# First key projection by both column halves of four token tiles, and wider spacing of the last attention batches, in a gated two-branch attention kernel

## The chip, the cores and the metric

The kernel runs on one core of a Trainium2 chip. The metric is the device time of one execution, in microseconds (us). Before the change it was 474.53 us, the median of three runs (474.02 to 475.82).

## The reference, cut to what matters

Two attention branches share one input and are mixed by a gate. Branch A is linear attention, branch B a local, dilated one. There are 2048 tokens, width 1024, and 32 heads of 32.

```python
x = A_x                                                # [1, 2048, 1024] bf16
g = sigmoid((x * gate_w).sum(-1, keepdims=True))
# A: q, k, v = split(x @ A_wqkv); phi(t) = where(t > 0, t + 1, exp(t)) + 1e-6
#    kv = phi(k)^T v per head; z = sum of phi(k); o = phi(q) kv / (phi(q) z); a = o @ A_wo
# B: q, k, v = split(x @ B_wqkv); each token attends to 8 earlier ones, 2 apart
#    softmax, times v; b = o @ B_wo
return g * a + (1 - g) * b
```

The change touches the first stage, phi(x @ A's key columns), and the end of branch B's attention, which is done in batches between other matmuls.

## The kernel before: the parts that matter

The keys of A are 2048 x 1024: 16 token tiles of 128 by two column halves of 512, each a sum over 8 steps of 128 (`kt`). That is 256 matmuls of 128 x 512. They need x transposed (`xT`), which DMA transposes bring, and the weights (`WkA[half]`). The loads are written like this:

```python
    WkA = [wpool.tile([P, KT, 512], BF16, name="WkA0", tag="wa")]

    def load_xT(k, t0, t1):
        nc.sync.dma_start_transpose(out=xT[:, 2 * k:2 * k + 2, t0 * P:t1 * P],
                                    in_=rows(x, t0 * P, t1 * P)[:, 2 * k * P:(2 * k + 2) * P])

    for k in range(4):
        (nc.sync if k else nc.scalar).dma_start(
            out=WkA[0][:, 2 * k:2 * k + 2, :],
            in_=A_wqkv[2 * k * P:(2 * k + 2) * P, D:D + 512].rearrange("(kt p) n -> p kt n", p=P))
        for t in (0, 4):
            load_xT(k, t, t + 4)
    for t in range(8, NB):
        nc.sync.dma_start_transpose(out=xT[:, :, t * P:(t + 1) * P], in_=rows(x, t * P, (t + 1) * P))
    WkA += load_w("WkA", A_wqkv, D, "wa", only=(1,))
    # ... the rows of x for the next stage, then more weights
```

The matmuls fill eight accumulation banks, one for each of the first eight token tiles, group `k` of two `kt` steps by group. The other tiles and the second half follow one bank at a time. `phi` empties a bank with one ScalarE exponential and two VectorE instructions.

```python
            warm_up(38)                  # matmuls on a tile of ones, results unused

            first = [bank_k(t) for t in range(8)]
            for k in range(4):
                for t in range(8):
                    for kt in (2 * k, 2 * k + 1):
                        project(first[t], t, kt, 0)
                    if k == 3:
                        phi(work, pk[:, t, 0:512], first[t])
            for half in range(2):
                for t in range(NB):
                    if half == 0 and t < 8:
                        continue
                    pj = bank_k(t)
                    for kt in range(KT):
                        project(pj, t, kt, half)
                    phi(work, pk[:, t, half * 512:(half + 1) * 512], pj)
```

Branch B's attention runs in 40 batches, `scores(g)` and later `pv(g)`, placed between the steps of other matmuls. A step is four 64 x 512 quadrant matmuls. `pv` writes the one `o2` tile, which VectorE has to empty (reciprocals, then multiplications) before the next `pv`.

```python
            for g, (c, m, n) in enumerate(BATCHES):
                p_ = 64 * c + ((43, 55, 75, 86, 97) if c < KT - 1 else (43, 55, 75, 81, 87))[m // 4]
                events.append((p_, lambda g=g: scores(g)))
                events.append((p_ + (14 if c < KT - 1 or m < 8 else 11), lambda g=g: pv(g)))
```

The softmax here doesn't subtract the row's maximum and nothing guards it: scores larger than these inputs give would overflow.

Of the kernel before, what the change touches and what calls it, by code (L numbers as in the profile page):

```python
# [10 lines left out]
BF16 = mybir.dt.bfloat16  # L11
F32 = mybir.dt.float32
# [3 lines left out]
P = 128  # L16
# [23 lines left out]
def kernel(  # L40
# [11 lines left out]
    nc = tc.nc  # L52
    S, D = A_x.shape[1:]
# [5 lines left out]
    def rows(ap, s0, s1):  # L59
        return ap[s0 // 1024, s0 % 1024:(s1 - 1) % 1024 + 1, :]  # L60
# [3 lines left out]
    KT = D // P  # L64
    NB = S // P
# [5 lines left out]
    wpool = ctx.enter_context(tc.tile_pool(name="wpool", bufs=2))  # L71
# [4 lines left out]
    def load_w(name, src, col0, tag, only=(0, 1)):  # L76
        halves = []
        for h in only:
            w = wpool.tile([P, KT, 512], BF16, name=f"{name}{h}", tag=tag)
            c0 = col0 + h * 512  # L80
            nc.sync.dma_start(out=w[:], in_=src[:, c0:c0 + 512].rearrange("(kt p) n -> p kt n", p=P))
            halves.append(w)
        return halves
# [4 lines left out]
    def load_rows(eng, t0, t1):  # L88
        eng.dma_start(out=xrow[:, t0:t1, :], in_=rows(x, t0 * P, t1 * P).rearrange("(t p) d -> p t d", p=P))

    WkA = [wpool.tile([P, KT, 512], BF16, name="WkA0", tag="wa")]

    def load_xT(k, t0, t1):
        nc.sync.dma_start_transpose(out=xT[:, 2 * k:2 * k + 2, t0 * P:t1 * P],  # L94
                                    in_=rows(x, t0 * P, t1 * P)[:, 2 * k * P:(2 * k + 2) * P])

    for k in range(4):
        (nc.sync if k else nc.scalar).dma_start(  # L98
            out=WkA[0][:, 2 * k:2 * k + 2, :],
            in_=A_wqkv[2 * k * P:(2 * k + 2) * P, D:D + 512].rearrange("(kt p) n -> p kt n", p=P))  # L100
        for t in (0, 4):
            load_xT(k, t, t + 4)
    for t in range(8, NB):
        nc.sync.dma_start_transpose(out=xT[:, :, t * P:(t + 1) * P], in_=rows(x, t * P, (t + 1) * P))
    WkA += load_w("WkA", A_wqkv, D, "wa", only=(1,))
    load_rows(nc.sync, 0, 4)
    for t in range(4, NB, 4):
        load_rows(nc.sync, t, t + 4)
# [34 lines left out]
    def phi(work, dst, pj):  # L143
        e = work.tile([P, 512], F32, name="e", tag="e")
        nc.scalar.activation(out=e[:], in_=pj[:], func=ACT.Exp)  # L145
        nc.vector.tensor_scalar(out=e[:], in0=e[:], scalar1=1.0, scalar2=1e-6, op0=ALU.min, op1=ALU.add)  # L146
        nc.vector.scalar_tensor_tensor(out=dst, in0=pj[:], scalar=0.0, in1=e[:], op0=ALU.max, op1=ALU.add)

    with tc.manual_schedule(engines={PE}):

        with ExitStack() as s1:
            ps_1 = s1.enter_context(tc.tile_pool(name="ps_1", bufs=4, space=bass.MemoryType.PSUM))
            junk = s1.enter_context(tc.tile_pool(name="junk", bufs=1))
            work = s1.enter_context(tc.tile_pool(name="work1", bufs=3))

            s1.enter_context(tc.manual_schedule(engines={DVE}))
            pk = big.tile([P, NB, D], BF16, name="pk", tag="pkO")
            def project(pj, t, kt, half):
                nc.tensor.matmul(pj[:], lhsT=xT[:, kt, t * P:(t + 1) * P], rhs=WkA[half][:, kt, :],  # L159
                                 start=(kt == 0), stop=(kt == KT - 1))  # L160

            def warm_up(n):
                warm = ps_1.tile([P, P], F32, name="warm", tag="p1")
                for i in range(n):
                    nc.tensor.matmul(warm[:], lhsT=onesb[:], rhs=onesb[:], start=True, stop=True)


            warm_up(38)

            def bank_k(t):  # L170
                return (ps_1.tile([P, 512], F32, name="pk1_ps", tag="p1") if t & 4 else
                        ps_pj.tile([P, 512], F32, name="pk_ps", tag="pj"))

            first = [bank_k(t) for t in range(8)]
            for k in range(4):
                for t in range(8):
                    for kt in (2 * k, 2 * k + 1):
                        project(first[t], t, kt, 0)
                    if k == 3:
                        phi(work, pk[:, t, 0:512], first[t])  # L180
            for half in range(2):
                for t in range(NB):
                    if half == 0 and t < 8:
                        continue
                    pj = bank_k(t)
                    for kt in range(KT):
                        project(pj, t, kt, half)
                    phi(work, pk[:, t, half * 512:(half + 1) * 512], pj)
# [8 lines left out]
            for t in range(1, NB):  # L197
                side.append(lambda t=t: nc.vector.tensor_tensor(
                    out=zacc[:], in0=zacc[:] if t > 1 else pk[:, 0, :], in1=pk[:, t, :], op=ALU.add))
            side.append(lambda: nc.gpsimd.partition_all_reduce(zrow[:], zacc[:], P, bass_isa.ReduceOp.add))  # L200
            for t in range(NB):
                side.append(lambda t=t: nc.vector.tensor_tensor_reduce(
                    out=gjunk[:], in0=xrow[:, t, :], in1=gw_row[:], scale=1.0, scalar=0.0, op0=ALU.mult,
# [3 lines left out]
            for half in range(2):  # L207
                g_ = junk.tile([P, KT, 512], BF16, name=f"G{half}", tag=f"G{half}")
                G.append(g_)
                for kt in range(KT):  # L210
                    pj = ps_pj.tile([P, 512], F32, name="g_ps", tag="pj")
# [142 lines left out]
        with ExitStack() as s2:  # L354
# [93 lines left out]
            def pv(g):  # L448
                c, m0, n = BATCHES[g]
                pt, base, ns = PT[g % 2], BLOCKS[m0][0], n // 2  # L450
                o2 = ps_o.tile([P, 2, 512], F32, name="o2", tag="o")[:, :, 0:ns * 132] \
                    .rearrange("p a (s i e) -> p a s i e", s=ns, i=4)
                for s_ in range(ns):
                    for i in range(4):
                        for dm in range(2):
                            for par in range(2):
                                m = m0 + 2 * s_ + dm
                                o = BLOCKS[m][0] - base
                                r = slice(64 * par, 64 * par + 64)
                                h = (dm + par) % 2  # L460
                                nc.tensor.matmul(o2[64 * h:64 * h + 64, par, s_, i, :], lhsT=pt[r, i, o:o + 64],  # L461
                                                 rhs=V[r, m, 4 * c + i, :], start=True, stop=True)
                part = m0 >= 8
                if m0 in (0, 8):
                    obs[part] = small.tile([P, 2, 5, P], BF16, name="Ob", tag="Ob")
                Ob = obs[part]
                s0 = m0 // 2 - 4 * part
                rd = small.tile([P, 2, 2, 4, 1], F32, name="rd", tag="rd")
                for a in range(2):
                    nc.vector.reciprocal(out=rd[:, a, 0:ns], in_=o2[:, a, :, :, Dh:Dh + 1])  # L470
                for a in range(2):
                    nc.vector.tensor_tensor(out=Ob[:, a, s0:s0 + ns, :].rearrange("p s (i e) -> p s i e", i=4),
                                            in0=o2[:, a, :, :, 0:Dh],
                                            in1=rd[:, a, 0:ns].broadcast_to([P, ns, 4, Dh]), op=ALU.mult)
                if m0 not in (4, 16):
                    return
                runs = ((0, 1), (1, 4), (2, 3)) if not part else ((8, 1), (9, 4), (10, 4), (17, 1))
                for par in range(2):
                    for m, k in runs:
                        h = (m + par) % 2  # L480
                        q0, w, _ = BLOCKS[m]
                        step = 2 * w if k > 1 else w
                        sl = m // 2 - 4 * part
                        nc.sync.dma_start(
                            out=obd[c][1024 * par + q0:1024 * par + q0 + k * step, :]
                            .rearrange("(s r) d -> r s d", r=step)[0:w],
                            in_=Ob[64 * h:64 * h + w, par, sl:sl + k, :])
                    if part and c == KT - 1:
                        nc.sync.dma_start_transpose(out=OBT[:, c, 1024 * par:1024 * par + 1024],
                                                    in_=obd[c][1024 * par:1024 * par + 1024, :])  # L490
                if part and c < KT - 1:
                    nc.sync.dma_start_transpose(out=OBT[:, c, :], in_=obd[c][0:S, :])

            events = []
            for g, (c, m, n) in enumerate(BATCHES):
                p_ = 64 * c + ((43, 55, 75, 86, 97) if c < KT - 1 else (43, 55, 75, 81, 87))[m // 4]
                events.append((p_, lambda g=g: scores(g)))
                events.append((p_ + (14 if c < KT - 1 or m < 8 else 11), lambda g=g: pv(g)))

            def between(a, b):  # L500
                return [(p_ - a, f) for p_, f in events if a <= p_ < b]
# [12 lines left out]
            for c in range(KT):  # L514
                kts[c] = kpool.tile([P, 2, 1024], BF16, name="kt", tag="kt")
                for hh in range(2):
# [3 lines left out]
                    if 1 <= c <= 2:  # L520
                        t = 2 * (c - 1) + hh
                        nc.sync.dma_start_transpose(out=pqT[0][:, :, t * P:(t + 1) * P],
                                                    in_=pqd[t * P:(t + 1) * P, :])
# [26 lines left out]
        with ExitStack() as s3:  # L550
# [44 lines left out]
            first = [out_part(i, *p_) for i, p_ in enumerate(parts[:7])]  # L595
# [3 lines left out]
            for i, p_ in enumerate(parts):  # L599
# [4 lines left out]
                f = out_part(i, *p_)  # L604
# [33 lines left out]
```

## Time and profile before

| what | value |
|---|---|
| time, median of 3 | 474.53 us |
| the execution that was profiled | 475.77 us, span 474.0 us |
| TensorE busy | 466.4 us of the span |
| first key matmul / next stage starts | 5.80 / 61.90 us |

The profile is of an execution 1.2 us longer than the median.

From the page of the profile of before, the shares of busy time and the chain of work that ended last. TensorE (PE) is nearly always busy, and the rest of the chain is the sync engine's queue (SPq) and a transfer.

```profile
PE 466.4 (98%) x5718; PEld 245.7 (52%) x5750; DVE 277.1 (58%) x601; ACT 168.7 (36%) x271; POOL 25.5 (5%) x88
...
PE 95%; SPq 3%; DMA 1%; issue 1%; ACT 0%
```

From the waits of TensorE in before (engine, line, what it waited for, then us in total, how often, the longest):

```profile
PE pk_ps L159 <- DMA xT<-in_A_x_dram: 0.9, 2, 0.5
PE o L461 <- issue: 0.5, 1, 0.5
```

From the timeline of before, 0 to 14 us (start, duration, engine, line, instruction; in brackets the idle time ahead of it and what ended it). The first two DMA transposes cost the sync engine 1.34 and 1.43 us to issue, and the first key matmul waits 0.45 us for the first of them.

```profile
0.80 2.83 SPq L94 DMA_TRANSPOSE xT<-in_A_x_dram  x2
...
1.12 4.23 PE L165 MATMUL warm<-onesb 128*128 128x128 bf16 x38 [1.12 <-DVE onesb L116]
3.67 0.58 SPq L98 DMA_DIRECT2D WkA<-in_A_wqkv_dram  x1
...
5.80 8.38 PE L159 MATMUL pk_ps<-WkA,xT 128*128 128x512 bf16 x37 [0.45 <-DMA xT<-in_A_x_dram]
```

From the same kernel's timeline of TensorE, 17 to 23 us: the second wait, for token tile 8.

```profile
20.29 2.98 PE L159 MATMUL pk_ps<-WkA,xT 128*128 128x512 bf16 x13 [0.48 <-DMA xT<-in_A_x_dram]
```

From the chain of before, 346 to 361 us (start, duration, what): the end of the attention. 0.54 us pass with no work ("issue": nothing that the profile shows is waited for) ahead of the last value matmuls (`o L461`).

```profile
346.88 0.20 PE s2b L438 x15
...
351.32 0.32 PE o L461 x32
351.64 1.31 PE q_ps L381 x24
352.95 0.54 issue
353.49 0.31 PE o L461 x16
353.80 6.49 PE q_ps L381 x120
360.29 0.32 PE d_ps L579
```

I use two distances below: from the first key matmul to the start of the next stage (`g_ps`), and from this `s2b` at 346.88 to the output stage's first `d_ps` at 360.29, here 13.41 us.

### The profile page before, as it was taken

Reading aid. Unit: us, or ns where it says so; the run is one execution under the profiler, and the core shown is the slowest. Engines: PE = TensorE matmul, PEld = TensorE weight load, DVE = VectorE, ACT = ScalarE, POOL = GpSimd, SP = SyncE. Lnnn points to the kernel's source line nnn. Section 1 sums busy time; section 2 is a strip of 40 time slices with the busy share of each in tenths; the row PEclk is TensorE's granted clock in tenths of the full one; section 3 lists DMA queues with packets and bytes.
Section 4 is the critical chain, followed back from the end, with each engine's and each line's share of the span. In section 5 each row is a group of like instructions: output and inputs, shape, how many; then the busy total and the mean of one; then the engine's idle time right before and its main releaser. Section 6 shows DMA issues by size and latency. Waiting matters only on the chain.

```text
span 474.0 us, 13165 instructions
## 1 busy us (share of the span) xinstructions
PE 466.4 (98%) x5718; PEld 245.7 (52%) x5750; DVE 277.1 (58%) x601; ACT 168.7 (36%) x271; POOL 25.5 (5%) x88
## 2 busy tenths in 40 slices
PE   8999999999999999999999999999999999999997
PEld 5444444445444444445666666666665444444444
DVE  0586689990329999999566676767660049800000
ACT  1343311102433333333555555555551134221121
POOL 2910000500000000001000000000000000000000
PEclk9999999999999999999999999999999999999999
DMA  8999980000644243627326525442563933221111
GB/s 184 189 260 374 347 267 0 0 1 0 215 127 110 93 139 130 154 96 240 112 56 108 104 59 85 99 90 56 92 166 71 198 91 78 68 55 45 34 34 45
DMA packets 98557, 55.41 MB, mean 117 GB/s; under 512 B 69826, under 2 KB 90434, under 8 KB 98498
## 3 DMA queue, kind: packets, MB, share of 16 engines
q1 hardware_dynamic: 93474, 50.10, 41.7%
q10 hardware_dynamic: 5024, 4.46, 2.9%
q8 instruction: 45, 0.74, 0.7%
q14 instruction: 14, 0.11, 0.1%
HBM read 26.10 MB, written 15.86 MB: 89 GB/s over the span
## 4 chain that ended last, share of the span: by engine, by line
PE 95%; SPq 3%; DMA 1%; issue 1%; ACT 0%
PE q_ps L381 26%; PE d_ps L579 12%; PE p_ps L288 12%; PE g_ps L213 12%; PE e_ps L579 11%; PE pk_ps L159 9%; PE p_ps L324 9%; SPq L94 2%; PE o L461 2%; PE s2b L438 2%; DMA xT<-in_A_x_dram 1%; PE kv_ps L233 0%; SPq L98 0%; PE w_ps L276 0%; ACT osb L584 0%
## 5 line engine op out<-in xcount | busy, mean ns | idle before, releaser
L381 PE MATMUL q_ps<-xT,WqB 64*64 64x512 bf16 x1024 | 68.3, 376 | 0.0
L381 PE MATMUL q_ps<-xT,WkB 64*64 64x512 bf16 x1024 | 67.9, 376 | 0.0
L146 DVE TENSOR_SCALAR e<-e 128x512 f32<-128x512 f32 x64 | 27.4, 428 | 64.9 <-ACT e L145 64.9
L288 PE MATMUL p_ps<-WvB,xT 128*128 128x512 bf16 x250 | 57.2, 379 | 0.5 <-issue 0.3
L159 PE MATMUL pk_ps<-WkA,xT 128*128 128x512 bf16 x251 | 55.4, 379 | 1.2 <-DMA xT<-in_A_x_dram 0.9
L213 PE MATMUL g_ps<-pk,xrow 128*128 128x512 bf16 x250 | 54.9, 379 | 0.3
L443 ACT ACTIVATE PT<-s2b 128x928 bf16<-128x928 f32 (+4 forms) x40 | 34.2, 854 | 46.1 <-PE s2b L438 46.1
L445 DVE TENSOR_TENSOR PT<-PT,mask 128x928 bf16<-128x928 bf16 (+4 forms) x40 | 23.6, 590 | 36.9 <-ACT PT L443 36.9
L324 PE MATMUL p_ps<-WqA,xT 128*128 128x512 bf16 x187 | 43.1, 379 | 0.3
L579 PEld LDWEIGHTS <-pqT 128*128 128x128 bf16 x264 | 25.8, 98 | 29.8 <-issue 0.4
L159 PEld LDWEIGHTS <-xT 128*128 128x128 bf16 x256 | 24.8, 98 | 31.5 <-DMA xT<-in_A_x_dram 2.0
L579 PEld LDWEIGHTS <-OBT 128*128 128x128 bf16 x264 | 25.8, 98 | 29.4
L213 PEld LDWEIGHTS <-xrow 128*128 128x128 bf16 x256 | 25.0, 98 | 30.2
L288 PEld LDWEIGHTS <-xT 128*128 128x128 bf16 x256 | 24.6, 98 | 30.0 <-issue 0.9
L381 PEld LDWEIGHTS <-WkB 64*64 64x64 bf16 x1024 | 32.3, 107 | 15.1 <-issue 0.6
L381 PEld LDWEIGHTS <-WqB 64*64 64x64 bf16 x1024 | 31.6, 107 | 15.2 <-issue 0.7
L145 ACT ACTIVATE e<-pk_ps 128x512 f32<-128x512 f32 x32 | 18.9, 597 | 41.6 <-PE pk_ps L159 36.6
L293 ACT CAST tmp<-p_ps 128x512 bf16<-128x512 f32 x32 | 18.8, 590 | 37.5 <-PE p_ps L288 31.2
L579 PE MATMUL d_ps<-WoA,pqT 128*128 128x512 bf16 (+1 forms) x133 | 31.1, 373 | 0.2
L579 PE MATMUL d_ps<-WoB,OBT 128*128 128x512 bf16 (+1 forms) x134 | 31.2, 373 | 0.1
L324 PEld LDWEIGHTS <-xT 128*128 128x128 bf16 x192 | 18.8, 98 | 22.7
L584 ACT ACTIVATE osb<-d_ps,omg 128x512 bf16<-128x512 f32 (+1 forms) x17 | 11.5, 674 | 50.1 <-PE d_ps L579 48.4
(62 smaller groups left out, 512.4 us busy)
## 6 DMA issues: line engine op xcount, KB each, us to landing
vd<-tmp SPq DMA_DIRECT2D x16, 264.0 KB
xrow<-in_A_x_dram SPq DMA_DIRECT2D x4, 1024.0 KB
out_dram<-osb ACTq DMA_DIRECT2D x31, 128.0 KB
pqd<-tmp SPq DMA_DIRECT2D x12, 256.0 KB
WvA<-in_A_wqkv_dram SPq DMA_DIRECT2D x2, 1024.0 KB
WoA<-in_A_wo_dram SPq DMA_DIRECT2D x2, 1024.0 KB
WvB<-in_B_wqkv_dram SPq DMA_DIRECT2D x2, 1024.0 KB
WqA<-in_A_wqkv_dram SPq DMA_DIRECT2D x2, 1024.0 KB
```

The source lines that it names most:

```text
L145: nc.scalar.activation(out=e[:], in_=pj[:], func=ACT.Exp)
L146: nc.vector.tensor_scalar(out=e[:], in0=e[:], scalar1=1.0, scalar2=1e-6, op0=ALU.min, op1=ALU.add)
L159: nc.tensor.matmul(pj[:], lhsT=xT[:, kt, t * P:(t + 1) * P], rhs=WkA[half][:, kt, :], start=(kt == 0), stop=(kt == KT - 1))
L213: nc.tensor.matmul(pj[:], lhsT=xrow[:, t, kt * P:(kt + 1) * P], rhs=pk[:, t, half * 512:(half + 1) * 512], start=(t == 0), stop=(t == NB - 1))
L288: nc.tensor.matmul(st["pj"][:], lhsT=xT[:, kt, t * P:(t + 1) * P], rhs=WvB[half][:, kt, :], start=(kt == 0), stop=(kt == KT - 1))
L293: nc.scalar.copy(out=v[:, half * 16:(half + 1) * 16, 0:Dh], in_=st["pj"][:].rearrange("p (h e) -> p h e", h=16))
L324: nc.tensor.matmul(st["pj"][:], lhsT=xT[:, kt, t * P:(t + 1) * P], rhs=WqA[half][:, kt, :], start=(kt == 0), stop=(kt == KT - 1))
L381: nc.tensor.matmul(banks[o][64 * j:64 * j + 64, :], lhsT=lhsT(r, kt, j), rhs=rhs(r, kt), start=first and kt == 0, stop=kt == KT - 1, skip_ ...
L443: nc.scalar.activation(out=pt[:, :, 0:W_], in_=s2b[:].rearrange("p a b s -> p (a b) s")[:, :, 0:W_], func=ACT.Exp, scale=SCALE)
L445: nc.vector.tensor_tensor(out=pt[:, :, 0:W_], in0=pt[:, :, 0:W_], in1=mask[:, None, base:base + W_].broadcast_to([P, 4, W_]), op=ALU.mult)
L579: nc.tensor.matmul(st["ps"][:, 0:n], lhsT=lhsT, rhs=W[c0 // 512][:, c, c0 % 512:c0 % 512 + n], start=(side == 0 and c == 0), stop=(side == ...
L584: nc.scalar.activation(out=osb[:, 0:n], in_=st["ps"][:, 0:n], func=ACT.Copy, scale=omg[:, tb:tb + 1])
```

## The change

Its intent is to start the first matmul on half as much x, to use each transposed piece for both column halves so that fewer transposes are needed early, and to give VectorE more time between the last batches. Four token tiles by two halves now fill the eight banks. The weights come in eight pieces. Eight steps and nine steps lie between the last batches in place of six and six.

```diff
--- before.py
+++ after.py
@@ -88,21 +88,27 @@
     def load_rows(eng, t0, t1):
         eng.dma_start(out=xrow[:, t0:t1, :], in_=rows(x, t0 * P, t1 * P).rearrange("(t p) d -> p t d", p=P))
 
-    WkA = [wpool.tile([P, KT, 512], BF16, name="WkA0", tag="wa")]
+    WkA = [wpool.tile([P, KT, 512], BF16, name=f"WkA{h}", tag="wa") for h in range(2)]
 
     def load_xT(k, t0, t1):
         nc.sync.dma_start_transpose(out=xT[:, 2 * k:2 * k + 2, t0 * P:t1 * P],
                                     in_=rows(x, t0 * P, t1 * P)[:, 2 * k * P:(2 * k + 2) * P])
 
-    for k in range(4):
-        (nc.sync if k else nc.scalar).dma_start(
-            out=WkA[0][:, 2 * k:2 * k + 2, :],
-            in_=A_wqkv[2 * k * P:(2 * k + 2) * P, D:D + 512].rearrange("(kt p) n -> p kt n", p=P))
-        for t in (0, 4):
-            load_xT(k, t, t + 4)
-    for t in range(8, NB):
+    def load_wk(eng, k, h):
+        eng.dma_start(out=WkA[h][:, 2 * k:2 * k + 2, :],
+                      in_=A_wqkv[2 * k * P:(2 * k + 2) * P, D + 512 * h:D + 512 * h + 512]
+                      .rearrange("(kt p) n -> p kt n", p=P))
+
+    load_wk(nc.scalar, 0, 0)
+    load_xT(0, 0, 2)
+    load_xT(0, 2, 4)
+    load_wk(nc.sync, 0, 1)
+    for k in range(1, 4):
+        load_wk(nc.sync, k, 0)
+        load_xT(k, 0, 4)
+        load_wk(nc.sync, k, 1)
+    for t in range(4, NB):
         nc.sync.dma_start_transpose(out=xT[:, :, t * P:(t + 1) * P], in_=rows(x, t * P, (t + 1) * P))
-    WkA += load_w("WkA", A_wqkv, D, "wa", only=(1,))
     load_rows(nc.sync, 0, 4)
     for t in range(4, NB, 4):
         load_rows(nc.sync, t, t + 4)
@@ -165,24 +171,23 @@
                     nc.tensor.matmul(warm[:], lhsT=onesb[:], rhs=onesb[:], start=True, stop=True)
 
 
-            warm_up(38)
-
-            def bank_k(t):
-                return (ps_1.tile([P, 512], F32, name="pk1_ps", tag="p1") if t & 4 else
+            warm_up(34)
+
+            def bank_k(i):
+                return (ps_1.tile([P, 512], F32, name="pk1_ps", tag="p1") if i & 4 else
                         ps_pj.tile([P, 512], F32, name="pk_ps", tag="pj"))
 
-            first = [bank_k(t) for t in range(8)]
+            first = [bank_k(i) for i in range(8)]
             for k in range(4):
-                for t in range(8):
-                    for kt in (2 * k, 2 * k + 1):
-                        project(first[t], t, kt, 0)
-                    if k == 3:
-                        phi(work, pk[:, t, 0:512], first[t])
-            for half in range(2):
-                for t in range(NB):
-                    if half == 0 and t < 8:
-                        continue
-                    pj = bank_k(t)
+                for half in range(2):
+                    for t in range(4):
+                        for kt in (2 * k, 2 * k + 1):
+                            project(first[4 * half + t], t, kt, half)
+                        if k == 3:
+                            phi(work, pk[:, t, half * 512:(half + 1) * 512], first[4 * half + t])
+            for t in range(4, NB):
+                for half in range(2):
+                    pj = bank_k(2 * t + half)
                     for kt in range(KT):
                         project(pj, t, kt, half)
                     phi(work, pk[:, t, half * 512:(half + 1) * 512], pj)
@@ -493,9 +498,9 @@
 
             events = []
             for g, (c, m, n) in enumerate(BATCHES):
-                p_ = 64 * c + ((43, 55, 75, 86, 97) if c < KT - 1 else (43, 55, 75, 81, 87))[m // 4]
+                p_ = 64 * c + ((43, 55, 75, 86, 97) if c < KT - 1 else (43, 55, 75, 83, 92))[m // 4]
                 events.append((p_, lambda g=g: scores(g)))
-                events.append((p_ + (14 if c < KT - 1 or m < 8 else 11), lambda g=g: pv(g)))
+                events.append((p_ + (14 if c < KT - 1 or m < 8 else 12), lambda g=g: pv(g)))
 
             def between(a, b):
                 return [(p_ - a, f) for p_, f in events if a <= p_ < b]
```

## The prediction

> **What bounds it now.** TensorE is busy 466.4 of 474.0 us (98%, busy table); the chain of waits is 95% TensorE, the rest nearly all in the first 20 us, where the sync engine issues DMA transposes of x. No matmul is added or removed, so only TensorE gaps can go. Timeline and waits show three:
>
> 1. The first real matmul starts at 5.80 us. 38 warm-ups run 1.12 to 5.35; then TensorE waits 0.45 us for the first transposed piece of x (four tiles x 256 columns; issue 0.80 to 2.14, landed 3.6 us later).
> 2. At 20.29 it waits 0.48 us for token tile 8, whose transpose is issued from 14.62 on, after eight 256 KB transposes and four weight pieces. Keys take 5.80 to 61.90 = 56.1 us for 256 x 0.2157 = 55.2.
> 3. In the last chunk, at 352.95, 0.54 us before the last value matmuls; their first weight load had waited until 352.75 for VectorE to empty the o2 bank. Batches are 6 steps (about 1.3 + 0.4 us) apart; VectorE needs 0.64 (mask) + 0.28 (reciprocals) + 0.76 (multiply) = 1.7 us each, plus 0.41 for look copies.
>
> **What the change does.** The first group needs half a transposed piece. Estimate from the issue durations: 0.67 us less issue, so landing near 5.0. The warm-up loses 4 x 0.107 us and ends near 4.9. The Trainium skill, "TensorE: Matmul & The Clock Gate", Part 1, puts the release of the clock after a busy window of about 3.4 us of varying phase. The trace agrees: warm-ups stay 0.107 us apart for 3.9 us, key matmuls 0.2157 from the first. An earlier start may leave one or two cold matmuls, 0.2 us each.
>
> Each transposed piece now feeds twice the matmuls: the first 13.8 us take 1 MB of transposes and 2 MB of plain weights, before 2 and 1. The DMA moves about 210 GB/s while transposing, 350 to 390 in plain loads, so the mix is easier. Issue ends for groups 1, 2, 3: near 4.9, 7.5, 10.2; plus 3.3 to 3.6 us to landing, as before: 8.4, 11.0, 13.7; needed at 8.5, 11.9, 15.4. Only group 1 is close (0 to 0.3 us). Later tiles are used for 3.45 us each and supplied every 1.5, so wait 2 goes. The rows of x come 1 to 2 us later, needed only at 60.
>
> Start 0.8, tile 8 0.5, less 0.1 to 0.2 of new waits: 1.1 us, all on the critical path.
>
> Last chunk: 8 to 9 steps (2.2 to 2.4 us) cover VectorE's 1.7; the gap goes, 0.5 us. The last value matmuls come 6 steps (1.3 us) later; the final transposes of OBT, issued at 362.3, move to about 363.5, needed near 374: free.
>
> **Prediction.** 474.53 - 1.6 = 472.9 us, range 472.0 to 474.2. Faster by over 2%: 0.01; within 2%: 0.98; slower: 0.01.
>
> **Signs.** First key matmul at 4.8 to 5.3; no TensorE wait on x's transposes between 16 and 25 us; G stage starts at 60.4 to 61.2 (was 61.90); TensorE gap in the last chunk under 0.2 us; output stage about 1.6 us earlier, length unchanged.
>
> **What would make it wrong.** Half a piece costs nearly as much issue as a whole one; group 1 starves; cold matmuls; the last gap is not the bank but something else ("issue") and stays; run spread (474.02 to 475.82).

## The result, and the profile after

| | before | after |
|---|---|---|
| median time | 474.50 us (4 runs, 474.02 to 475.82) | 474.64 us (4 runs, 474.57 to 475.01) |
| ratio | | 1.000, 95% interval 0.998 to 1.0021 |
| profiled execution: time, span | 475.77, 474.0 | 474.62, 472.8 |
| first key matmul | 5.80 us | 4.72 us |
| next stage starts | 61.90 us | 61.44 us |
| `s2b` to first `d_ps` | 13.41 us | 12.60 us |

A ratio is the mean time of one kernel's fast runs over that of the other's of the same rounds, so it is not quite the ratio of the medians quoted. The two profiles differ by 1.2 us; the timed runs show no difference, within an interval of about 1 us either way. So two questions stand. Why do the profiles show a gain that the runs do not, and why did the keys stage gain so little where the first matmul starts 1.1 us earlier?

From the page of after:

```profile
PE 468.1 (99%) x5746; PEld 245.4 (52%) x5746; DVE 276.9 (59%) x601; ACT 168.6 (36%) x271; POOL 25.4 (5%) x88
...
PE 98%; DMA 1%; SPq 1%; ACT 0%; issue 0%
```

From the timeline of TensorE in after, 0 to 30 us. The first key matmul is early, but the ninth, the first of the second column half, starts at 7.75 us after a wait for weights.

```profile
4.72 2.52 PE L165 MATMUL pk_ps<-WkA,xT 128*128 128x512 bf16 x8
7.75 22.61 PE L165 MATMUL pk_ps<-WkA,xT 128*128 128x512 bf16 x104 [0.51 <-DMA WkA<-in_A_wqkv_dram]
```

From the timeline of the sync engine in after, 0 to 40 us: two half pieces take 2.60 us to issue, nearly as long as two whole ones in before (2.83).

```profile
0.80 2.60 SPq L94 DMA_TRANSPOSE xT<-in_A_x_dram  x2
3.44 1.09 SPq L98 DMA_DIRECT2D WkA<-in_A_wqkv_dram  x2
4.58 1.24 SPq L94 DMA_TRANSPOSE xT<-in_A_x_dram  x1
```

From the chain of after, 0 to 64 us. It no longer starts at the transposes of x but goes through a weight piece, the second of the two issued from 3.44 us on; from 7.75 us on 248 matmuls run without a gap.

```profile
0.80 1.30 SPq L94
...
2.16 1.24 SPq L94
...
3.44 0.58 SPq L98
...
4.08 3.63 DMA WkA<-in_A_wqkv_dram
...
7.75 53.69 PE pk_ps L165 x248
```

From the timeline of the weight loads (PEld) in after, 4.5 to 8.6 us. They are 0.43 us apart at first, where they are 0.2157 apart later: the first matmuls run on half the clock. (The clock line of a page does not show this: this trace's first clock record, of the full clock, begins at 5.99 us, and nothing is recorded ahead of it.)

```profile
5.15 0.15 PEld L165 LDWEIGHTS <-xT 128*128 128x128 bf16 x1 [0.28 <-issue]
5.57 0.15 PEld L165 LDWEIGHTS <-xT 128*128 128x128 bf16 x1 [0.28 <-issue]
6.00 0.96 PEld L165 LDWEIGHTS <-xT 128*128 128x128 bf16 x5 [0.27 <-issue]
```

From the chain of after, 346 to 361 us: no gap before the last value matmuls.

```profile
346.43 0.20 PE s2b L443 x15
...
351.51 0.25 PE o L466 x30
351.76 1.95 PE q_ps L386 x34
353.71 0.12 PE o L466 x15
353.84 5.20 PE q_ps L386 x96
359.03 1.83 PE d_ps L584 x8
```

### The profile page after: what moved, and what is told of

Read it like the earlier page. It is cut to its first block, busy times and chain, and to the rows that moved or that the text cites. A ratio compares the mean times of both kernels' runs of the same rounds, so it can differ in the third digit from the quotient of the medians.

```text
span 472.8 us, 13192 instructions
## 1 busy us (share of the span) xinstructions
PE 468.1 (99%) x5746; PEld 245.4 (52%) x5746; DVE 276.9 (59%) x601; ACT 168.6 (36%) x271; POOL 25.4 (5%) x88
## 4 chain that ended last, share of the span: by engine, by line
PE 98%; DMA 1%; SPq 1%; ACT 0%; issue 0%
PE q_ps L386 26%; PE d_ps L584 12%; PE p_ps L293 12%; PE g_ps L218 12%; PE pk_ps L165 11%; PE e_ps L584 11%; PE p_ps L329 9%; PE o L466 2%; PE s2b L443 2%; DMA WkA<-in_A_wqkv_dram 1%; SPq L94 1%; PE kv_ps L238 0%; PE w_ps L281 0%; SPq L98 0%; ACT osb L589 0%
```

## The experiments

All kernels gave correct results. Each time below is the median of a kernel's runs; "before" of the same rounds had medians of 474.81 (first four kernels), 475.04 (next four) and 474.77 us (last four). The three rounds ran on different chips, so a kernel is compared with before of its own round. The intervals of the ratios are 0.6 to 1.1 us either way; differences of a few tenths are read from the traces, mostly one for each kernel.

"The second half's first weight piece" or "urgent piece" is the load `load_wk(nc.sync, 0, 1)`, which key matmul 9 needs.

### First round: is the profile of before a usual one, and which part does what?

**e1_before_again: no edit.**

> The kernel before, unchanged, for a second profile of it. Theory A (the profile of before that the prediction was read from was of an execution 1.3 us longer than its usual 474.5 us, and part of the gaps read there are not in a usual execution): span near 472.7, and at least one of the three gaps (0.45 us before the first key matmul, 0.48 us at token tile 8, 0.54 us before the last value matmuls) is missing or under 0.15 us. Theory B (the gaps are in every execution, and the new kernel pays an equal new cost elsewhere): all three gaps there again within 0.1 us each. Time 474.5 either way, ratio 1.000.

Measured: 474.75 us, ratio 1.0002 (0.9989 to 1.0015), span 472.9. From its chain, around token tile 8 (0 to 64 us) and at the end of the attention (346 to 365 us):

```profile
19.21 0.59 PE pk_ps L159 x2
19.80 0.01 issue
19.81 10.32 PE pk_ps L159 x47
...
61.43 1.08 PE g_ps L213 x5
```

```profile
346.43 0.20 PE s2b L438 x16
...
350.87 0.32 PE o L461 x32
351.19 1.31 PE q_ps L381 x24
352.50 0.12 PE o L461 x16
352.62 6.49 PE q_ps L381 x120
359.11 0.32 PE d_ps L579
```

The gap at tile 8 is 0.01 us, and the gap before the last value matmuls is not there. The first matmul starts at 5.72 (before: 5.80). The same kernel reaches the next stage at 61.43 instead of 61.90 and takes 12.68 us at the end of the attention instead of 13.41. In this trace, too, the first weight load of the last value matmuls waited for VectorE to empty the bank, 0.28 us, and TensorE lost nothing by it, since matmuls issued earlier were still running. So theory A holds in its main point: two of the three gaps that I meant to remove are not in every execution.

**e2_keys_only: the new keys stage, the old spacing.**

```diff
-... else (43, 55, 75, 83, 92))[m // 4]        # after
+... else (43, 55, 75, 81, 87))[m // 4]        # as before; pv 11 steps later, not 12
```

> The new keys stage with the old spacing of the last chunk. Trace of after: its first key matmul starts at 4.72, but the second half's first weight piece lands at 7.71, so that 248 of 256 matmuls start at 7.75, as if the stage had started at 6.03 without gaps; before starts at 5.80 with a 0.48 us gap at tile 8. Theory B: the keys stage ends 0.4 to 0.5 us earlier than before, time 474.0 to 474.2. Theory A with the tile 8 gap absent in usual executions: the stage ends 0 to 0.3 us later than before, time 474.4 to 474.9.

Measured: 474.90 us (six runs), ratio 1.0011 (0.9997 to 1.0024). Its first key matmul starts at 4.72, the ninth at 8.00, the next stage at 61.68: 0.25 us later than in e1. The end of the attention takes 12.67 us, with the old spacing and no gap. The new keys stage alone gains nothing against an execution of before that has no gap at tile 8.

**e3_spacing_only: the old keys stage, the new spacing.**

```diff
-... else (43, 55, 75, 81, 87))[m // 4]
-... or m < 8 else 11)
+... else (43, 55, 75, 83, 92))[m // 4]
+... or m < 8 else 12)
```

> The old keys stage with only the new spacing in the last chunk. Theory B (gap of 0.54 us and some 0.27 us more around it in every execution): 0.5 to 0.8 us faster, 473.7 to 474.0. Theory A (this gap was only in that profile): 0 to 0.2 us faster, 474.3 to 474.5. In its trace no TensorE gap before the last value matmuls.

Measured: 474.66 us, ratio 1.0003 (0.9991 to 1.0015). The end of the attention takes 12.60 us, against 12.68 in e1 and 12.67 in e2. The new spacing is worth 0.08 us in a usual execution.

**e4_wk01_act: after, the urgent piece issued by the scalar engine.**

```diff
     load_wk(nc.scalar, 0, 0)
+    load_wk(nc.scalar, 0, 1)
     load_xT(0, 0, 2)
     load_xT(0, 2, 4)
-    load_wk(nc.sync, 0, 1)
```

> After, with the second half's first weight piece issued by the scalar engine right behind the first half's, instead of by the sync engine behind two transposes of 1.30 and 1.24 us issue each. If the wait at 7.2 to 7.75 us is the cost of that issue order, it goes, the keys stage ends 0.5 us or more earlier than in after (61.44), near 60.9 with the cold matmuls of after left, 60.4 if the clock comes up in time; time 0.5 to 1.0 us under after, 473.6 to 474.1. If the rival holds (the DMA can't bring more by then, whatever the order), the wait stays or moves to the third and fourth token tile, and the time stays at 474.6.

Measured: 474.09 us (six runs, one of them 476.95, so the ratio 0.9998 has a wide interval, 0.998 to 1.0016). The wait for weights is gone, and the next stage starts at 61.15. But the first key matmul now waits for x:

```profile
5.45 24.83 PE L165 MATMUL pk_ps<-WkA,xT 128*128 128x512 bf16 x111 [0.53 <-DMA xT<-in_A_x_dram]
```

(This is its timeline of TensorE, 0 to 30 us.) The weight piece on the other queue takes time from the transposed piece. The Trainium skill, "DMA: Bandwidth & Descriptors", section "Issuing engines are not separate DMA queues", says that DMAs of all engines run on the same 16 DMA engines and interleave. This agrees: the transposed piece landed at 5.41 us in place of 4.57, and 4.72 became 5.45.

### Second round: why does the urgent piece come late?

My theory C here was that the split costs an issue of 1.24 us, which pushes the weight piece back.

**f1_after_again: no edit of after.**

> The changed kernel once more, for a second trace of it and its time beside the three below. If its wait for the second half's first weight piece belongs to the order of issue and not to one odd execution, key matmul 9 starts again at 7.7 to 8.0 us, whatever the clock did before it, and the next stage starts at 61.4 to 61.7. Time 474.5 to 474.9, ratio to before 0.999 to 1.001.

Measured: 474.61 us (474.57 to 474.86), ratio 0.9991 (0.998 to 1.0003). From its timeline of TensorE, 0 to 20 us:

```profile
4.72 2.00 PE L165 MATMUL pk_ps<-WkA,xT 128*128 128x512 bf16 x8
7.78 12.46 PE L165 MATMUL pk_ps<-WkA,xT 128*128 128x512 bf16 x56 [1.06 <-DMA WkA<-in_A_wqkv_dram]
```

The clock came up sooner in this execution (the weight loads are 0.2157 us apart from 5.05 on), so the first eight matmuls were done earlier and the wait is longer: 1.06 instead of 0.51 us. The ninth starts at 7.78 all the same, and the next stage at 61.47. Everything before the ninth matmul is slack: 248 x 0.2157 = 53.5 us after 7.78 is 61.3, and the rest is small gaps.

**f2_whole_first: after, with the first transposed piece whole.**

```diff
-    load_xT(0, 0, 2)
-    load_xT(0, 2, 4)
+    load_xT(0, 0, 4)
     load_wk(nc.sync, 0, 1)
```

> After, with the first transposed piece whole again (one issue in place of two, the rest as in after). Theory C (a half piece costs the sync engine as much issue as a whole one, 1.30 and 1.24 us, so the split delays the weight piece behind it, and the early start is lost in a wait): weight piece issued at 2.2 in place of 3.44, landing near 6.4, first key matmul at 5.5 to 5.7, no wait after it, next stage at 60.9 to 61.4, time 0.1 to 0.5 us under after. Rival (the start of the first matmul sets the stage's end): the first matmul comes 0.9 us later than in after, so the next stage does too: 62.3, time 475.4.

Measured: 474.48 us, ratio 0.9988 (0.9975 to 1.0002). The next stage starts at 61.56, so the rival (62.3) is out. But theory C is out too. From its timeline of TensorE, 0 to 20 us:

```profile
4.95 1.90 PE L164 MATMUL pk_ps<-WkA,xT 128*128 128x512 bf16 x8 [0.36 <-DMA xT<-in_A_x_dram]
7.88 12.46 PE L164 MATMUL pk_ps<-WkA,xT 128*128 128x512 bf16 x56 [1.02 <-DMA WkA<-in_A_wqkv_dram]
```

From its chain, 0 to 64 us, the wait for the urgent piece, from its issue to its landing at 7.83:

```profile
2.80 5.03 DMA WkA<-in_A_wqkv_dram
```

The sync engine came to its weight pieces 1.25 us earlier (2.19 instead of 3.44), and the urgent piece landed no earlier (7.83 instead of 7.71). And the whole piece of x landed for a start at 4.95, where the same whole piece in before lets the first matmul start at 5.80 and in e1 at 5.72. What differs is the piece issued behind it: there another transposed one, here a plain one. That this is the reason is not shown.

**f3_wk01_pool: after, the urgent piece issued by GpSimd.**

```diff
-    load_wk(nc.sync, 0, 1)
...
+    load_wk(nc.gpsimd, 0, 1)
     mask = consts.tile([P, S // 2], BF16, name="mask")
```

> After, with the second half's first weight piece issued by the GpSimd engine ahead of its mask, neither behind the transposes (after) nor next to the first weights on the scalar engine's queue (where it delayed the first transposed piece's landing from 4.6 to 5.4 us). If the piece then lands between 5.5 and 6.4: first key matmul at 4.7 to 5.1, no wait at 7.2 to 7.7, next stage at 60.4 to 61.0 (by how late the clock rises), time 473.5 to 474.1. If any early load of this piece delays the first transposed piece by its own 0.7 us: the first matmul at 5.4 and all as in the scalar engine's version, 61.15 and 474.1.

Measured: 483.92 us, ratio 1.0189. Neither branch happened. The scheduler placed the load behind GpSimd's first mask instruction, which waits until 9.39 us, so the load was issued at 9.59 and key matmul 9 started at 14.98. It says nothing about an early load. The loss (9.3 us against after) is more than the 7.2 us by which the matmul came later: the clock fell while TensorE stood idle, and the first seven matmuls after it took 3.15 us.

**f4_whole_act: the whole piece, and both first weight pieces from the scalar engine.**

```diff
     load_wk(nc.scalar, 0, 0)
+    load_wk(nc.scalar, 0, 1)
-    load_xT(0, 0, 2)
-    load_xT(0, 2, 4)
-    load_wk(nc.sync, 0, 1)
+    load_xT(0, 0, 4)
```

> After, with the first transposed piece whole and both first weight pieces issued by the scalar engine: against the scalar engine's version with the split piece (first matmul 5.45, next stage 61.15, 474.09 us) this tells what the split alone is worth once the weight piece isn't behind it. If the half piece is worth its smaller transfer: first matmul 5.8 to 6.3 here, next stage 61.4 to 61.9, time 474.4 to 474.9. If it's worth nothing: 61.0 to 61.2 and 474.0 to 474.2.

Measured: 474.67 us (six runs, two of them 476.16 and 477.95), ratio 1.0007 (0.9984 to 1.003). First matmul 6.23, next stage 61.66, both in the range of "worth its smaller transfer". Where a weight piece is in flight beside it, the half piece starts the stage 0.8 us earlier.

### What the compiled kernel showed

f2 sent me to the list of instructions that the compiled kernel of after really has. The sync engine's first loads are these (`WkA0` is the first half, `WkA1` the second; the first half's group 0 is issued by the scalar engine):

```
1 L94 DmaTransposeAnt xT_70<-in_A_x_dram 128x2x256 x2
2 L98 DMACopy WkA0_72<-in_A_wqkv_dram 128x2x512
3 L98 DMACopy WkA1_73<-in_A_wqkv_dram 128x2x512
4 L94 DmaTransposeAnt xT_70<-in_A_x_dram 128x2x512
```

The program lists `load_wk(nc.sync, 0, 1)` first and `load_wk(nc.sync, 1, 0)` second. The scheduler, which is free to order the sync engine's loads at this place, swapped them: group 1's first half, needed after 16 matmuls, goes ahead of group 0's second half, needed after 8. The same swap is in the compiled kernel of f2. This is what the chain above shows as "the second of the two". The trace also records the semaphores that tell of each load's landing: of the two pieces, the less urgent one landed at 6.94 in after and 7.06 in f2, the urgent one at 7.71 and 7.83. In f2, 480 of the 512 packets of both pieces had been moved by 6.46 us; the last 17 follow one after another, 0.04 us apart, until 7.38, as on a single engine that is behind the others. I read this so: the urgent piece shares the engines with the other, and it has landed only when its slowest engine is through, which is about when both pieces are done. The packed trace doesn't tell a packet's engine or piece, so this reading is not shown. The Trainium skill, "DMA: Bandwidth & Descriptors", section "Two DMAs through the same engine are not ordered", says that nothing orders DMAs across the 16 engines; the packets here, moved from 4.2 to 7.4 us for the two pieces' 0.5 MB, are in keeping with that but can't show it.

### Third round: the order alone

For these the sync engine's loads are put in a region where the scheduler keeps the program's order. To close the region cleanly, the load of the gate's row moved into it, and the warm-up's tile of ones lies in another buffer to make room. Neither is on the path.

**g1_order_fixed: after, with the loads issued in the order of the program.**

```diff
+    with tc.manual_schedule(engines={SP}):
         load_wk(nc.scalar, 0, 0)
         load_xT(0, 0, 2)
         load_xT(0, 2, 4)
         load_wk(nc.sync, 0, 1)
         # ... all further loads of this place, indented, unchanged
+        gw_row = consts.tile([P, D], BF16, name="gw_row")
+        nc.sync.dma_start(out=gw_row[:], in_=gate_w.partition_broadcast(P))
```

> After, with the sync engine held to the order in which the program lists its loads. In the compiled kernel of after the scheduler had swapped two of them: it issues the first half's weights of group 1 (needed at 8.2) ahead of the second half's of group 0 (needed at 6.4). Theory D (this swap makes the wait: two 256 KB pieces share the DMA engines, and the urgent one lands last): the urgent piece is issued at 3.44 in place of 4.08 and lands at 6.3 to 6.8; key matmul 9 at 6.5 to 7.0 in place of 7.75 (later only where the clock is still low); next stage at 60.2 to 61.0; time 473.4 to 474.1. Theory E (DMA throughput alone sets the landing; the order of two neighbouring pieces doesn't matter): key matmul 9 at 7.5 to 8.0, next stage 61.4, 474.6. (The row of gate weights is allocated elsewhere and the warm-up's ones lie in another buffer, so that the order could be fixed; neither is on the path.)

Measured: 474.30 us (473.89 to 474.38), ratio 0.9987 (0.9975 to 1.0). From its timeline of TensorE, 0 to 20 us, and of the weight loads, 0 to 10 us:

```profile
4.75 15.33 PE L168 MATMUL pk_ps<-WkA,xT 128*128 128x512 bf16 x64
```

```profile
5.15 0.15 PEld L168 LDWEIGHTS <-xT 128*128 128x128 bf16 x1 [0.28 <-issue]
...
6.86 0.15 PEld L168 LDWEIGHTS <-xT 128*128 128x128 bf16 x1 [0.28 <-issue]
7.19 2.90 PEld L168 LDWEIGHTS <-xT 128*128 128x128 bf16 x14 [0.18 <-issue]
```

No wait for weights is left in this trace, but the order is not the whole reason. By the landing semaphores the urgent piece landed at 7.12 us and the other at 7.85, where after has 7.71 and 6.94. So theory E (the order does not matter) is out, and theory D has the direction right but not the size: it expected a landing at 6.3 to 6.8. On the full clock the eight matmuls ahead would be done at 4.75 + 8 x 0.2157 = 6.48, so about 0.7 us of wait would be left (an estimate from these numbers). No wait shows because the low clock kept those eight busy until 7.62, where key matmul 9 starts. The next stage starts at 61.31, not at 60.2 to 61.0, and the time is 0.2 us above what I expected. Without any gap, 4.75 + 256 x 0.2157 would be 59.97. Of the missing 1.3 us, 1.1 are the first six matmuls, which take 2.4 us in place of 1.3 before the clock has come up at about 7.2 us; the rest is small gaps. What the early start gains is mostly spent at half speed.

**g2_whole_order: the same, with the first transposed piece whole.**

```diff
-        load_xT(0, 0, 2)
-        load_xT(0, 2, 4)
+        load_xT(0, 0, 4)
```

> The same with the first transposed piece whole (one issue fewer ahead of the weights). Theory D: urgent piece issued at 2.2, landing at 5.6 to 6.4 (in the version with a whole piece and the swap it landed at 7.83), first key matmul at 4.95 to 5.3, no wait after it, next stage 60.4 to 61.0, time 473.5 to 474.1, within 0.2 of the split one, so the split is worth nothing. Theory E: wait until 7.8 as in the swapped one, 474.5.

Measured: 473.94 us (473.78 to 474.21), ratio 0.9982 (0.997 to 0.9995). First matmul 4.76, no wait after it, low clock until 6.85, next stage 61.19 (expected 60.4 to 61.0; again the clock). The urgent piece landed at 6.78 (7.83 in f2, which differs in the order and not in the pieces), later than the 5.6 to 6.4 that I expected; key matmul 9 started at 7.50. The split of the first piece is worth nothing once the order is right. This kernel beats before by 0.8 us of median in the same rounds. After did not run in these rounds.

**g3_order_late: order held, the urgent piece moved behind group 1's x.**

```diff
-        load_wk(nc.sync, 0, 1)
         for k in range(1, 4):
             load_wk(nc.sync, k, 0)
             load_xT(k, 0, 4)
+            if k == 1:
+                load_wk(nc.sync, 0, 1)
             load_wk(nc.sync, k, 1)
```

> Order held too, but the second half's piece of group 0 moved one transpose further back, behind group 1's x. A dose: if the landing of this piece sets the end of the stage (248 of 256 matmuls start after it), it's issued near 5.4 and lands near 8.6 to 9.2, so the next stage comes at 62.3 to 63.0, 0.9 to 1.5 us after that of after, and the time is 475.4 to 476.2. If it doesn't set it: 474.6 as in after.

Measured: 477.78 us, ratio 1.0054 (1.004 to 1.0068). From its timeline of TensorE, 0 to 20 us:

```profile
4.68 1.90 PE L169 MATMUL pk_ps<-WkA,xT 128*128 128x512 bf16 x8
9.91 2.14 PE L169 MATMUL pk_ps<-WkA,xT 128*128 128x512 bf16 x7 [3.32 <-DMA WkA<-in_A_wqkv_dram]
```

The direction is as expected, the size is not: the piece landed at 9.86, 0.7 us later than the latest I expected, and the next stage started at 65.28. A second cost came on top. After an idle stretch of 3.3 us the weight loads are 0.43 us apart again from 11.41 to 14.40. The times agree: the two runs with a granted clock of 1.000 took 476.57 and 477.15 us, the three with 0.996 took 477.78 to 478.50. The Trainium skill, "TensorE: Matmul & The Clock Gate", Part 1, says that the clock falls back to half after an idle window of about 3.4 us. In f3 this agrees: TensorE was idle from 6.90 us on, and the clock record falls at 11.96. In g3 it agrees only roughly: the idle stretch (6.58 to 9.91) was 3.32 us, and the record falls at 10.97, 1.06 us after the matmuls had begun again.

**g4_before_third: no edit of before, one look.**

> The kernel before, a third look. If the gaps of 0.48 us at token tile 8 and 0.54 us before the last value matmuls are of odd executions only (absent in the second look, in the one with the old last chunk, and in the one with the old keys), at least one of them is absent here too; span 472.5 to 473.7.

Measured: 474.99 us, span 473.3 (one run, so its state is unknown). The gap at tile 8 is there again, 0.43 us at 20.25 (put down to VectorE there, but the weight load ahead of it had waited 0.92 us for x). The gap before the last value matmuls is not, and the end of the attention takes 12.67 us.

### The traces side by side

| trace | first key matmul | largest gap after it | next stage | `s2b` to `d_ps` | span |
|---|---|---|---|---|---|
| before | 5.80 | 0.48 (tile 8) | 61.90 | 13.41 | 474.0 |
| e1 (= before) | 5.72 | none | 61.43 | 12.68 | 472.9 |
| g4 (= before) | 5.83 | 0.43 (tile 8) | 61.86 | 12.67 | 473.3 |
| e3 (old keys) | 5.55 | none | 61.50 | 12.60 | 472.9 |
| after | 4.72 | 0.51 (weights) | 61.44 | 12.60 | 472.8 |
| f1 (= after) | 4.72 | 1.06 (weights) | 61.47 | 12.60 | 472.8 |
| e2 (new keys) | 4.72 | 0.23 (weights) | 61.68 | 12.67 | 473.1 |
| g1 (order held) | 4.75 | none | 61.31 | 12.60 | 472.7 |
| g2 (order held, whole piece) | 4.76 | none | 61.19 | 12.59 | 472.5 |

The old keys stage reaches the next one at 61.43 to 61.90 (mean of four 61.67), the new one at 61.44 to 61.68 (mean of three 61.53).

## Why the prediction was wrong, point by point

The prediction was 472.9 us with a range of 472.0 to 474.2; the measured median is 474.64. The change was forecast to gain 1.6 us and gained 0 to 0.4 us (ratios 1.000 and 0.9991 in two sets of rounds; both intervals hold 1, and neither holds the 0.9966 of the forecast).

- **The step that failed first: "the gap goes, 0.5 us" and "tile 8 0.5" as gains of every execution.** I summed gaps of one profile, of an execution of 475.77 us, and took the sum off a median of 474.53. Of four traces with the old keys stage, two have the gap at tile 8. Of four with the old spacing (before, e1, g4, e2), one has the gap before the last value matmuls. No trace of the new keys stage has the first, and none with the new spacing the second; since only one of the four old ones had the second, that the new spacing removes it is not shown. In the rounds of f1 the runs of after spread less (474.57 to 474.86) than those of before (474.20 to 476.00). This is in keeping with gaps that are gone, but a timed run without a trace can't show which gap it had.
- **The mechanism of the last gap was wrong too.** VectorE's work of 1.7 us a batch does hold back a weight load by 0.28 us (e1), but TensorE doesn't lose it. In before, too, that weight load waited 0.28 us and started at 352.75, ahead of the gap (352.95 to 353.49), so the bank was free by then. The new spacing is worth 0.08 us (12.68 to 12.60), not 0.5. What the 0.54 us of "issue" in before's profile were stays open.
- **"Start 0.8" failed.** The first matmul came at 4.72, in the range of the sign I gave (4.8 to 5.3) or a little better. It was worth nothing, because I checked the landings of groups 1, 2 and 3 and not that of group 0's second half, which is needed first. It landed at 7.71, where the eight matmuls ahead of it would be done at 6.45 on the full clock. From there on the stage is as if it had started gapless at 7.75 - 8 x 0.2157 = 6.02, later than the 5.80 of before.
- **Why it landed there:** in part because the scheduler had swapped it with a less urgent piece. g1 and g2 put the order right and nothing else of weight, and it landed 0.6 us earlier than in after (7.12) and 1.05 us earlier than in f2 (6.78); g3 moved it back and the wait grew. I had read the program's order from the source, and the swap is not to be seen there. The order does not explain all of it: 7.12 and 6.78 are still later than 6.5, when the eight matmuls would be done on the full clock.
- **"0.67 us less issue" was wrong:** half a piece takes 1.30 us to issue, a whole one 1.34. I had listed this among what would make the prediction wrong. It happened and was not the cause: f2 saves that issue and waits just as long.
- **"One or two cold matmuls, 0.2 us each" was too small.** In after the low clock hides inside the wait. In g1, where the wait is gone, it costs 1.1 us, over six matmuls. The clock came up at anything from 4.0 (g4) to 7.1 us (g1) by the traces' own clock records, with no order by kernel (before had 5.8, e1 4.2). This and the landing limit what mending the order can give. In the times it is not clear: against before of the same rounds the medians are 0.43 us lower in f1, 0.47 in g1 and 0.83 in g2, and the intervals of the three ratios overlap.
- **Right:** the wait at tile 8 is in none of the traces of the new keys stage, the supply of later groups and tiles holds, the next stage's rows of x come early enough, and the final transposes of the attention's output cost nothing. The class (within 2%) was right.

Left open: why the scheduler swapped the two loads; why the urgent piece still lands at 6.8 to 7.1 us in the right order; why tile 8's transpose comes late in some executions; and the "issue" gap.

## What to carry to other kernels

Before summing gaps of a profile into a forecast, compare the profiled execution's own time with the median, and take a second profile of the same kernel: a gap that comes and goes is worth its share of the runs only. When a first stage is fed by DMA, write down the landing that each of its first matmuls needs, in the order of the compiled instructions and not of the source, and check the piece needed first, not only the next groups. An earlier start is worth only what the clock lets it do: here TensorE ran at half speed until 4.0 to 7.1 us, and a wait that is gone from a trace may be hidden by this and not mended.

## What the Trainium skill lacked or had wrong

- "TensorE: Matmul & The Clock Gate", Part 1, puts the change of clock at around 4 us of sustained matmuls, plus or minus 0.5 us, and elsewhere says that the window of about 3.4 us runs freely and that the number of slow matmuls changes from run to run. Here warm-ups started at 1.12 us in every trace, and in the thirteen that have a clock record the clock rose at 4.0 (g4) to 7.1 us (g1), which is 2.9 to 6.0 us after them. The spread, 3.1 us, is nearly that of a whole free-running window, not of 0.5 us.
- "DMA: Bandwidth & Descriptors" gives a sequencer time for a DMA transpose out of HBM only for small tiles (631 cycles on earlier generations, in a table about another chip), not for pieces like these. Here a piece of 128 KB took 1.24 to 1.30 us of the sync engine and one of 256 KB 1.22 to 2.80 us over all traces (1.34 for the first in before), so halving a piece halved nothing; a plain piece of 256 KB took 0.58 us.
- The same page says that DMAs are not ordered across the engines, but not what this costs a small urgent load. Here the same transposed piece, issued at the same time, let the first matmul start at 5.55 to 5.83 us with another transposed piece behind it (before, e1, e3, g4), and at 4.95 and 4.76 with a plain one behind it (f2, g2); and a weight piece issued as the second of two landed as late with an issue at 2.8 us (7.83, f2) as with one at 4.08 (7.71, after), but at 6.78 (g2) and 7.12 (g1) as the first of the two.
